# A fused adaLN block: w_qkv as one transfer of whole rows, w_in by halves of its rows, both folds transposed ahead of the modulation, and a new order of all steps

## The chip, the cores and the metric

The kernel runs on one core of a Trainium2 chip. A core has five engines that run their own instruction queues side by side: TensorE (PE, matmuls and their weight loads), VectorE (DVE), ScalarE (ACT), GpSimd (POOL) and SyncE (SP, which here only issues transfers). Transfers are moved by 16 DMA engines; a transfer stands in the queue of the engine that issues it (SP or ACT here). Engines wait for each other through semaphores. The metric is the device time of one execution in microseconds (us); all times below are in us unless marked ns.

## What is computed

Two blocks on a sequence of 2048 tokens with 448 features, each behind a layer norm that is modulated by a conditioning vector c, and gated into the residual:

```
mod = silu(c) @ w_mod                     # six vectors of 448: sa ca ga sb cb gb
h = layernorm(x) * (1 + ca) + sa
q, k, v = split(h @ wqkv)                 # 16 heads of 28
phi(t) = [softmax(t @ w_phi), softmax(-(t @ w_phi))]        # per head
kv = phi(k)^T v ;  z = sum over tokens of phi(k)
o = phi(q) kv / (phi(q) z + 1e-6)
x = x + ga * (o @ wo)
h = layernorm(x) * (1 + cb) + sb
z1, z2 = split(gelu(h @ w_in))            # 896 columns each
g = w_sp @ layernorm(z2) + b_sp           # mixes over the 2048 tokens
x = x + gb * ((z1 * g) @ w_out)
```

All inputs are bfloat16; sums are kept in float32.

## The kernel before

The program has a fast path, which is what runs here, and a general path behind a flag that is read near the end; nothing of the general path runs. In the fast path (`fast_path`) the 2048 tokens are 16 tiles of 128. Its steps are small Python functions, each of which issues a few instructions for one tile or one block, and a string, `ORDER`, lists every step of the whole program in the order of issue. An engine's queue is just the steps of that string that use it, in that order. A word is a step's name, its numbers, the engine where there is a choice (`/V` VectorE, `/S` ScalarE, `/G` GpSimd, `/Y` SP) and the PSUM bank that it writes (`@A0` to `@A2` are pairs of banks, `@B0`, `@B1` single ones). There are only these five, so a step that wants a bank waits until the step that reads its last content is done.

The program has these stages:

- **The head.** `ld:` words issue the loads: tiles of x (`x0` to `x5`), w_qkv, the columns of w_mod for the shift and scale of the first block (`wsa`, `wca`), `phi`. `du` issues warm-up matmuls on zeros (lines 720 to 725), whose result nobody reads. `ct` and `ce` turn c into a column and take its silu. `csA`/`ccA` multiply it with w_mod into the columns of the shift and the scale (`esA`/`ecA` copy them out of PSUM). The modulation is not applied to the tokens but folded into the weights, and w_phi is folded into the q and k parts of w_qkv: `FTk`/`FTq` transpose the raw k and q weights on TensorE (16 transposes of 112x112 each), `ETk`/`ETq` copy them out, `PFk`/`PFq` multiply them with the block-diagonal w_phi (`bd`), `EPk`/`EPq` scale the rows by 1 + ca on the way out of PSUM. `FSk`/`FSq` and `FCk`/`FCq` make the row that the shift adds. For v, `SHv` makes the shift's row and `SCv` scales the weights in place. `X` and `XE` turn the first four normalised tiles on TensorE; later tiles are turned by transposing transfers (`T1`).
- **Keys and values.** Per tile, layer norm statistics on VectorE (`l1s`: L843, L844), then `kM`, `vM` (matmuls), the two exponentials on ScalarE (`kF`, `kE`), the sums and reciprocals on VectorE (`kS`, `kR`), the normalisation (`kP`), and `kA`, which adds the tile into the 16 small key-value products. `qM`, `qE`, `qF` make the features of q for 512 tokens at a time. `gr` and `ge` make the gates' rows.
- **The middle.** Per tile, `nM` (numerator and denominator), `nX`, `nC`, `nS`, `nT`, `nA` (division and sum of the two halves), a transposing transfer `T2`, `wM`/`wN` (times wo), `wR` (evacuates and adds the residual), `wQ` (squares), the second layer norm `l2R`, `l2r`, `l2a` for pairs of tiles, a transposing transfer `T3`, and then the first product of the second block: `zM` (z2, with `zG` gelu, `zQ` squares, `zR`, `zW`, `zN` normalisation) and `yM` (z1 for 512 tokens and 128 columns, with `yG` gelu). `SHw` and `SCw` fold shift and scale into w_in. `wN` is `wM` with one more matmul (line 994) that adds x through the identity, so that ScalarE can evacuate; without it, `wR` on VectorE adds x.
- **The token mix.** `P` steps multiply w_sp (loaded transposed by the `W` transfers) with z2, seven products where eight blocks would be plain, with sums of blocks prepared by `sS` and `tT`; `d` and `x` evacuate on VectorE and GpSimd; `oM`, `oE`, `oD` multiply with w_out, add the residual and store.

The steps that the change and the prediction touch are `FTk`/`FTq` (from line 801), `ET`, `PF`, `EP`, `SH`, `SC`, `load_rows` (line 642), the table of loads (line 650) and `ORDER` (line 482).

## Time and profile before

| | before |
|---|---|
| median of 3 runs | 253.3 (252.15 to 253.48) |
| the profiled execution: its own time | 252.36 |
| its span (first to last instruction) | 250.5 |
| DMA moved in the span | 25.2 MB |
| HBM read, written | 8.87 MB, 1.84 MB |

The span ends when the last store has landed. In the rows of a timeline stand the start, the duration, the engine, the line, the operation with its tiles and the number of instructions merged into the row; in brackets, how long the engine idled before it and who released it. [...] In the rows of windows, for each stretch, stand the length, the busy time and the count of instructions for PE, PEld (weight loads), DVE, ACT and POOL, the granted TensorE clock (1.00 is full), the mean busy share of the DMA engines, and GB/s.

### The profile page before, as it was taken

The page shows a single profiled execution, that of the slowest core. Times are in us where ns is not written, and L with a number is a line of the kernel's source. Part 1 is how long each engine was busy: PE and PEld are TensorE (multiplying, and loading weights), DVE is VectorE, ACT ScalarE, POOL GpSimd, SP SyncE. Part 2 cuts the span into 40 slices and gives each one's busy share as a digit, 9 for nine tenths or more (in the row PEclk, how much of TensorE's full clock was granted, in tenths as well). Part 3 has the DMA queues.
Part 4 walks back from the last instruction along what each step waited for, and adds up shares of the span by engine and source line. Part 5 has one row for each costly group of instructions (what it writes and reads, how often), then busy time and mean ns, then how long its engine had stood idle before and what let it go on. Part 6 is the DMA issues. An engine that isn't in the chain of part 4 may idle for free.

```text
span 250.5 us, 4157 instructions
## 1 busy us (share of the span) xinstructions
PE 243.3 (97%) x1517; PEld 127.0 (51%) x1517; DVE 185.4 (74%) x371; ACT 104.2 (42%) x220; POOL 125.2 (50%) x166
## 2 busy tenths in 40 slices
PE   7999999999999999999999999999999999999993
...
PEclk9889999999999999999999999999999999999999
...
GB/s 176 267 245 154 104 111 257 178 190 1 94 155 139 153 125 177 131 145 219 136 171 1 179 160 41 3 0 0 0 3 38 0 0 3 55 0 37 18 79 82
DMA packets 68655, 25.22 MB, mean 101 GB/s; under 512 B 58129, under 2 KB 68498, under 8 KB 68626
## 3 DMA queue, kind: packets, MB, share of 16 engines
...
HBM read 8.87 MB, written 1.84 MB: 43 GB/s over the span
## 4 chain that ended last, share of the span: by engine, by line
PE 77%; DVE 12%; POOL 4%; DMA 3%; issue 1%; ACT 1%; DVEq 0%; POOLq 0%
PE g_ps L1115 29%; PE o_ps L1150 8%; PE z_ps L1069 7%; PE z_ps L1040 7%; PE g_ps L1136 6%; PE x_ps L996 3%; DVE f_ksum L891 3%; PE v_ps L885 3%; DVE f_st L843 3%; PE k_ps L877 2%; PE q_ps L932 2%; PE kvacc L908 2%; PE num L960 2%; PE warm_ps L725 2%; DMA f_hT<-f_xpad 2%; DMA f_ar<-f_ar 1%
## 5 line engine op out<-in xcount | busy, mean ns | idle before, releaser
L1124 DVE TENSOR_TENSOR f_zb<-g_ps,f_zb 128x512 f32<-128x512 f32 (+1 forms) x31 | 20.3, 668 | 18.5 <-PE g_ps L1115 18.1
L1115 PEld LDWEIGHTS <-f_z2n 128*128 128x128 bf16 x192 | 18.8, 98 | 22.5
L1131 POOL TENSOR_TENSOR f_z1T<-f_zb,f_z1T 128x512 bf16<-128x512 f32 (+1 forms) x11 | 12.0, 1102 | 35.6 <-DVE f_zb L1124 35.6
L1040 PE MATMUL z_ps<-f_ar,f_hT 112*128 112x448 bf16 (+1 forms) x128 | 26.7, 352 | 0.5 <-DMA f_hT<-f_xpad 0.5
L1069 PE MATMUL z_ps<-f_hT,f_ar 113*128 113x512 bf16 (+1 forms) x112 | 26.4, 378 | 0.1
L1150 PE MATMUL o_ps<-f_wout,f_z1T 128*128 128x448 bf16 x112 | 22.5, 352 | 0.0
L1115 PE MATMUL g_ps<-f_ar 128*128 128x512 bf16 x96 | 22.2, 379 | 0.0
L1131 POOL TENSOR_TENSOR f_z1T<-f_Sx,f_z1T 128x512 bf16<-128x512 f32 x6 | 7.3, 1221 | 26.4 <-DVE f_Sx L1124 26.4
L937 ACT ACTIVATE f_Eq<-q_ps 112x1024 bf16<-112x1024 f32 x16 | 16.2, 1037 | 6.5 <-PE q_ps L932 6.5
L1072 ACT ACTIVATE f_z1T<-z_ps 128x512 bf16<-128x512 f32 x28 | 15.9, 594 | 6.0 <-PE z_ps L1069 5.8
L1040 PEld LDWEIGHTS <-f_hT 112*128 112x128 bf16 (+1 forms) x128 | 11.9, 97 | 12.8 <-DMA f_hT<-f_xpad 2.0
L1044 ACT ACTIVATE f_zb<-z_ps 128x896 bf16<-128x896 f32 x16 | 14.6, 915 | 6.8 <-PE z_ps L1040 3.7
L980 DVE TENSOR_TENSOR f_ar<-num,f_w 128x896 bf16<-128x896 f32 x16 | 17.1, 1087 | 0.5
L1069 PEld LDWEIGHTS <-f_ar 113*128 113x128 bf16 (+1 forms) x112 | 10.8, 97 | 12.9 <-issue 0.4
L880 ACT ACTIVATE f_E<-k_ps 128x448 bf16<-128x448 f32 x32 | 16.0, 558 | 2.7 <-DVE f_phik L898 2.0
L891 DVE TENSOR_REDUCE f_ksum<-f_E 128x32 f32<-128x896 bf16 x16 | 16.6, 1051 | 0.1
L1115 PE MATMUL g_ps<-f_Eq,f_z2n 128*128 128x512 bf16 x72 | 16.7, 379 | 0.0
L1150 PEld LDWEIGHTS <-f_z1T 128*128 128x128 bf16 x112 | 10.9, 98 | 10.7
L1153 DVE TENSOR_TENSOR f_xpad<-o_ps,f_x 128x448 bf16<-128x448 f32 x16 | 9.8, 620 | 8.0 <-PE o_ps L1150 6.8
L877 PE MATMUL k_ps<-f_Wk,f_hT 113*128 113x448 bf16 (+1 forms) x64 | 15.4, 366 | 0.0
L1115 PEld LDWEIGHTS <-f_ar 128*128 128x128 bf16 x96 | 9.4, 98 | 11.2
L932 PE MATMUL q_ps<-f_hT,f_Wq 113*128 113x512 bf16 (+1 forms) x64 | 15.0, 379 | 0.0
...
## 6 DMA issues: line engine op xcount, KB each, us to landing
...
f_ar<-in_B_w_in_dram ACTq DMA_DIRECT2D x2, 784.0 KB, 5.8
...
f_x<-in_A_x_dram SPq DMA_DIRECT2D x2, 448.0 KB, 8.8
f_wmg<-in_w_mod_dram ACTq DMA_DIRECT2D x2, 392.0 KB, 4.3
f_wout<-in_B_w_out_dram SPq DMA_DIRECT2D x1, 784.0 KB, 5.8
...
f_x<-in_A_x_dram ACTq DMA_DIRECT2D x1, 448.0 KB, 7.3
```

The lines of the kernel that those rows point to most:

```text
L877: nc.tensor.matmul(t[:, 0, 0:D], lhsT=hT[0:KR[m], i, m, :], rhs=Wk[0:KR[m], m, :], start=(m == 0), stop=(m == KC - 1))
L880: nc.scalar.activation(out=Er[i % NR][:, s, :], in_=ps["k" + str(i)][:, 0, 0:D], func=ACT.Exp, scale=1.0 - 2.0 * s)
L891: nc.vector.tensor_reduce(out=ksum[:, i], in_=Er[i % NR][:].rearrange("p s (c f h) -> p (s c) h f", c=4, h=HP), axis=AX.X, op=ALU.add)
L932: nc.tensor.matmul(t[:, u, :], lhsT=Wq[0:KR[m], m, cc * CB:cc * CB + P], rhs=hT[0:KR[m], 4 * st:4 * st + 4, m, :], start=(m == 0), stop=(m ...
L937: nc.scalar.activation(out=Eq[st // 2][0:CB, 2 * c2:2 * c2 + 2, s, (st % 2) * 512:(st % 2 + 1) * 512], in_=ps["q" + str(n)][0:CB, :, :], f ...
L980: nc.vector.tensor_tensor(out=tr[i % 2][:], in0=numv(i)[:, :, :, 0:DH], in1=wr[i // 2 % 2][:, i % 2].unsqueeze(3).to_broadcast([P, 2, H, D ...
L1040: nc.tensor.matmul(t[:, hf, 0:D], lhsT=hT[0:KR[m], i, m, :], rhs=win_s[0:KR[m], m, FH + hf * D:FH + (hf + 1) * D], start=(m == 0), stop=(m ...
L1069: nc.tensor.matmul(t[:, 0, :], lhsT=win_s[0:KR[m], m, fc * P:(fc + 1) * P], rhs=hT[0:KR[m], 4 * st:4 * st + 4, m, :], start=(m == 0), stop ...
L1115: nc.tensor.matmul(g, lhsT=sta[:, m, :], rhs=mov[:, m, :], start=(m == 0 and i in (1, 6, 7)), stop=(m == 7), skip_group_check=True)
L1124: nc.vector.tensor_tensor(out=o, in0=x, in1=y, op=ALU.add)
L1131: eng.tensor_tensor(out=z, in0=T[r][:, c0:c1], in1=z, op=ALU.mult)
L1150: nc.tensor.matmul(ps["o" + str(t)][:, 0, 0:D], lhsT=later["z1T"][:, FO[n], t * P:(t + 1) * P], rhs=wout_s[:, FO[n], :], start=(n == 0), s ...
```

## The change

Three loads (`wk`, `wv`, `wq`: 392 KB each, pieces of 896 bytes out of rows of 2688) become one, `wqkv` (1176 KB, whole rows), into one tile of which the three old names are views. The two halves of w_in are halves of its rows (`win0` the first two blocks of 112 rows with all 1792 columns, `win1` the other two), not halves of its columns. The step `dm` (nine small dummy matmuls in the middle) is gone. `wM` adds the identity matmul exactly when ScalarE evacuates; there are four such tiles now, and were seven. The string `ORDER` is new from the first word to the last.

```diff
-ORDER = """du:2@A1 ld:wk/S ld:x1/Y l1s:1 l1e:1,2/V l1r:1,2 tbl du:3@A2 ld:c/S du:3@A0 m1/G ld:x0/Y ld:wsa/Y m2a/V du:3@B1 du:14@A1 m4 ld:phi/Y du:3@B0 l1s:0 ct@B0
...
+ORDER = """ld:x0/S l1s:0 du:1@A0 m2b/V m1/G du:2@B1 du:1@B0 du:1@A1 du:2@B0 du:1@A0 du:1@A1 du:8@A2 l1e:0,1/V l1r:0,1 l1a:0/V tbl du:8@A1 ld:c/S ld:wqkv/Y ct@A2 ce:1
+ce:2 ce:3 m4 ce:4 du:4@B0 du:2@B0 ld:wsa/Y ld:phi/Y FTq:1@A1 FTk:1@B1 FTk:0@A2 ETk:1/V ld:x1/Y FTq:0@B0 ETq:1/S ld:wca/Y csA@A0 du:1@B1 du:2@B1 m3 du:1@A1
...
-    wk_raw = aph.tile([P, KC, D], BF, name="f_wk_raw")
-    wq_raw = aph.tile([P, KC, D], BF, name="f_wq_raw")
-    wv = aph.tile([P, KC, D], BF, name="f_wv")
+    wqkv = aph.tile([P, KC, 3 * D], BF, name="f_wqkv")
+    wq_raw, wk_raw, wv = (wqkv[:, :, n * D:(n + 1) * D] for n in range(3))
...
-        "wk": lambda q: load_rows(q, wk_raw[0:CB], A_wqkv[:, D:2 * D]),
-        "wv": lambda q: load_rows(q, wv[0:CB], A_wqkv[:, 2 * D:3 * D]),
-        "wq": lambda q: load_rows(q, wq_raw[0:CB], A_wqkv[:, 0:D]),
+        "wqkv": lambda q: load_rows(q, wqkv[0:CB], A_wqkv),
...
-        "win0": lambda q: load_rows(q, win_s[0:CB, :, 0:FH], B_w_in[:, 0:FH]),
-        "win1": lambda q: load_rows(q, win_s[0:CB, :, FH:2 * FH], B_w_in[:, FH:2 * FH]),
+        "win0": lambda q: load_rows(q, win_s[0:CB, 0:2], B_w_in[0:2 * CB]),
+        "win1": lambda q: load_rows(q, win_s[0:CB, 2:4], B_w_in[2 * CB:]),
...
-    def dm(n, i):
-        for _ in range(n):
-            nc.tensor.matmul(ps["n" + str(i)][:, 1, 480:512], lhsT=zero[:, 0:P], rhs=zero[:, 0:32], start=True, stop=True)
...
-"wM": lambda i, slot: wM(i, slot, False), "wN": lambda i, slot: wM(i, slot, True),
+"wM": lambda i, slot, eng: wM(i, slot, eng is nc.scalar),
```

What this does to the engines' queues is seen at three places. The first is the start of SP's queue, the loads. Before (f_wm1 are the columns of w_mod, first shift, then scale):

```order
L655 DMA f_x_74<-in_A_x_dram 128x448
L654 DMA f_x_74<-in_A_x_dram 128x448
L650 DMA f_wm1_117<-in_w_mod_dram 112x4x464
L647 DMA f_phi_114<-in_A_w_phi_dram 112x4x28
L656 DMA f_x_74<-in_A_x_dram 128x2x448
L650 DMA f_wm1_117<-in_w_mod_dram 112x4x464
L643 DMA f_wv_113<-in_A_wqkv_dram 112x4x448
L643 DMA f_wq_raw_112<-in_A_wqkv_dram 112x4x448
L657 DMA f_x_74<-in_A_x_dram 128x4x448
```

The same place now:

```order
L643 DMA f_wqkv_111<-in_A_wqkv_dram 112x4x1344
L650 DMA f_wm1_115<-in_w_mod_dram 112x4x464
L647 DMA f_phi_112<-in_A_w_phi_dram 112x4x28
L655 DMA f_x_74<-in_A_x_dram 128x448
L650 DMA f_wm1_115<-in_w_mod_dram 112x4x464
L656 DMA f_x_74<-in_A_x_dram 128x2x448
L657 DMA f_x_74<-in_A_x_dram 128x4x448
```

All of w_qkv goes first on SP (the k part had been first on ScalarE's queue), and the columns of w_mod, w_phi and all tiles of x but the first (which moved to ScalarE's queue) stand behind it.

The second place is VectorE's queue around the scale of the first block, f_ca1. Before, from the silu (f_scol) on (a few rows between are left out in both):

```order
L749 TENSOR_TENSOR f_scol_132<-f_e_131,ct_ps_212 112x4
L843 BN_STATS f_st1_143<-f_x_74 128x6
L844 BN_AGGR f_mv1_139<-f_st1_143 128x2
L767 CAST f_Ga_118<-cf_ps_255 112x4
L694 COPY f_Gb_119<-f_ident_73 112x112
L815 CAST f_wTk_135<-fs_ps_285 112x4
L764 TENSOR_SCALAR f_ca1_134<-cf_ps_305 112x4
L787 TENSOR_SCALAR f_Wk_109<-pf_ps_324,f_ca1_134 112x448
L787 TENSOR_SCALAR f_Wk_109<-pf_ps_347,f_ca1_134 112x448
L787 TENSOR_SCALAR f_Wk_109<-pf_ps_335,f_ca1_134 112x448
L787 TENSOR_SCALAR f_wv_113<-f_wv_113,f_ca1_134 112x448
```

The same place now (f_wTk and f_wTq are the transposed raw weights, f_st0 and f_st1 the statistics of tiles of x):

```order
L747 TENSOR_TENSOR f_scol_130<-f_e_129,ct_ps_199 112x4
L813 COPY f_wTk_133<-tps_234 112x2x448
L692 COPY f_Ga_116<-f_ident_73 112x112
L765 CAST f_Ga_116<-cf_ps_265 112x4
L813 COPY f_wTq_134<-tps_254 112x2x448
L762 TENSOR_SCALAR f_ca1_132<-cf_ps_325 112x4
L841 BN_STATS f_st1_141<-f_x_74 128x6
L842 BN_AGGR f_mv1_137<-f_st1_141 128x2
L841 BN_STATS f_st0_140<-f_x_74 128x6
L785 TENSOR_SCALAR f_wqkv_111<-f_wqkv_111,f_ca1_132 112x448
L785 TENSOR_SCALAR f_Wk_109<-pf_ps_393,f_ca1_132 113x448
```

VectorE copies both folds' transposes out ahead of the scale; between the scale and its share of the v weights stand the statistics of two tiles, and it evacuates one of the eight fold results instead of three.

The third place is ScalarE's queue from the silu of c on. Before:

```order
L813 COPY f_wTk_135<-tps_220 112x2x448
L813 COPY f_wTk_135<-tps_243 112x2x448
L813 COPY f_hT_75<-xt_ps_279 128x512
L783 ACTIVATE f_Wk_109<-pf_ps_341,f_ca1_134 113x448
L659 DMA f_x_74<-in_A_x_dram 128x4x448
L783 ACTIVATE f_wv_113<-sh_ps_353,f_ca1_134 113x448
L783 ACTIVATE f_wv_113<-f_wv_113,f_ca1_134 112x448
L880 ACTIVATE f_E0_121<-k_ps_361 128x448
```

Now, from the scale's first use to the first exponential (f_E0):

```order
L781 ACTIVATE f_wqkv_111<-sh_ps_307,f_ca1_132 113x448
L811 CAST f_wTk_133<-fs_ps_346 112x4
L781 ACTIVATE f_Wk_109<-pf_ps_320,f_ca1_132 112x448
L781 ACTIVATE f_Wk_109<-pf_ps_315,f_ca1_132 112x448
L781 ACTIVATE f_Wq_110<-pf_ps_383,f_ca1_132 112x448
L781 ACTIVATE f_Wk_109<-pf_ps_388,f_ca1_132 112x448
L886 CAST f_vaug_124<-v_ps_399 128x16x28
L811 CAST f_wTq_134<-fs_ps_417 112x4
L781 ACTIVATE f_Wq_110<-pf_ps_408,f_ca1_132 112x448
L811 COPY f_hT_75<-xt_ps_443 128x512
L811 COPY f_hT_75<-xt_ps_458 128x512
L781 ACTIVATE f_Wq_110<-pf_ps_449,f_ca1_132 113x448
```

Before, the first exponential of the keys stood right behind the scaled v weights, and the q fold came later, between the exponentials; now all but one of the fold results of k and q, and two turned tiles, stand ahead of it.

90 lines of the change are left out of this document (45 added, 45 removed).

## The prediction

> **What bounds the kernel now.** I read the page's busy shares and slices first, then TensorE's timeline row by row, then the windows of the places where it loses time, then the transfers and the groups by line.
>
> ```profile
> PE 243.3 (97%) x1517; PEld 127.0 (51%) x1517; DVE 185.4 (74%) x371; ACT 104.2 (42%) x220; POOL 125.2 (50%) x166
> ...
> PE   7999999999999999999999999999999999999993
> ...
> PEclk9889999999999999999999999999999999999999
> ```
>
> TensorE is full in every slice but the first and the last, so the end is its first useful matmul, plus the work, plus whatever it loses on the way: idle time, filler matmuls and time at a lowered clock. The dip of the clock in slices 2 and 3 is the only one. The timeline of TensorE shows the losses one by one (start, duration, line, count, idle before it):
>
> ```profile
> 1.23 4.74 PE L725 MATMUL warm_ps<-f_zero 128*128 128x256 bf16 x28 [1.23 <-DVE f_zero L683]
> ...
> 6.27 0.62 PE L809 MATMUL tps<-f_ident,f_wk_raw 112*112 112x112 bf16 x8
> ...
> 8.20 0.54 PE L760 MATMUL cf_ps<-f_scol,f_wm 112*128 112x1 bf16 x16 [0.58 <-DVE f_scol L749]
> ...
> 11.16 1.68 PE L774 MATMUL sh_ps<-f_wv,f_Ga 112*128 112x448 bf16 x4
> 12.62 1.70 PE L877 MATMUL k_ps<-f_Wk,f_hT 113*128 113x448 bf16 x4
> 14.12 1.21 PE L809 MATMUL tps<-f_ident,f_wq_raw 112*112 112x112 bf16 x16
> ...
> 15.39 0.93 PE L877 MATMUL k_ps<-f_Wk,f_hT 113*128 113x448 bf16 x4
> 16.15 0.94 PE L826 MATMUL fs_ps<-f_Ga,f_wq_raw 112*112 112x1 bf16 x16
> ...
> 38.32 0.59 PE L908 MATMUL kvacc<-f_vaug,f_phik 128*128 128x116 bf16 x8 [0.35 <-DVE f_phik L898]
> ...
> 112.66 1.69 PE L1040 MATMUL z_ps<-f_ar,f_hT 113*128 113x448 bf16 x8 [0.25 <-DMA f_hT<-f_xpad]
> ...
> 116.27 1.69 PE L1040 MATMUL z_ps<-f_ar,f_hT 113*128 113x448 bf16 x8 [0.20 <-DMA f_hT<-f_xpad]
> ...
> 235.45 10.76 PE L1150 MATMUL o_ps<-f_wout,f_z1T 128*128 128x448 bf16 x56
> ```
>
> Useful work starts at 6.27 (the first fold transposes; what precedes is filler and the tiny transposes of c) and ends at 246.2. Four matmuls with 448 columns take 0.76 from start to start at full clock (15.39 to 16.15). The two groups at 11.16 and 12.62 take 2.96 instead of 1.52: the clock was halved there, and with part of the transposes behind them that is a loss of **1.6**. Waits lose 1.1 before 11.2 (0.58 for the silu of c, and handovers of some 0.1 each), 0.5 around 38.3, and some 1.9 between 60 and 118 in pieces like the last two bracketed ones. Behind 138 there is nothing to win:
>
> ```profile
> 138.00:246.30 108.30, 108.21 (x515) 50.13 (x513) 70.76 (x98) 2.06 (x4) 38.41 (x23) 1.00 0.16 38
> ```
>
> TensorE (first figure behind the length) is busy for 108.21 of 108.30.
>
> **The change, part by part.** The sum is made in the profiled execution, 252.36 (span 250.5), which lies 0.9 under the median of the three runs; I add the same difference to the median.
>
> *Where the work starts.* Before, the k part of w_qkv came alone and first; now the folds wait for all of it.
>
> ```profile
> f_wk_raw<-in_A_wqkv_dram ACTq DMA_DIRECT2D x1, 392.0 KB, 4.3
> f_wv<-in_A_wqkv_dram SPq DMA_DIRECT2D x1, 392.0 KB, 6.1
> f_wq_raw<-in_A_wqkv_dram SPq DMA_DIRECT2D x1, 392.0 KB, 7.2
> ...
> f_ar<-in_B_w_in_dram ACTq DMA_DIRECT2D x2, 784.0 KB, 5.8
> ...
> f_x<-in_A_x_dram SPq DMA_DIRECT2D x1, 448.0 KB, 8.0
> ```
> ```profile
> 0.72 0.42 ACTq L643 DMA_DIRECT2D f_wk_raw<-in_A_wqkv_dram  x1
> ...
> 5.00 0.31 SPq L643 DMA_DIRECT2D f_wv<-in_A_wqkv_dram  x1
> 5.35 0.49 SPq L643 DMA_DIRECT2D f_wq_raw<-in_A_wqkv_dram  x1
> 5.89 0.68 SPq L657 DMA_DIRECT2D f_x<-in_A_x_dram  x1
> ...
> 47.12 0.33 ACTq L643 DMA_DIRECT2D f_ar<-in_B_w_in_dram  x1
> ...
> 49.86 0.32 ACTq L643 DMA_DIRECT2D f_ar<-in_B_w_in_dram  x1
> ```
>
> Issue plus time to landing: k at 5.0, v at 11.1, q at 12.6, the next 448 KB of x at 13.9. By 5.0, 392 KB of weights and the first 112 KB of x are in. Now 1176 KB of w_qkv and 112 KB of x must be in: 784 KB more. A half of w_in is just 784 KB, and its second half landed 2.7 behind the first; by the rows of v and q (392 KB in 1.5) it is 2.9, by that of x (448 KB in 1.3) 2.3. So it lands between 7.3 and 7.9; rows of 2688 bytes have no row here, the nearest are w_in's 1792, and x, whose rows lie one behind the other as these do, is faster: I take **7.5**, and 7.0 to 8.1 for the range. Filler covers TensorE up to about 6.5 (31 of the warm-up matmuls stand ahead, against 28 in 4.75), then it idles. Start: **+1.2**. All loads behind it on SP move back too: by the same rates the shift columns land near 9.1, x's second tile at 9.6, the scale columns (949 KB behind w_qkv) near 11.1 and the third and fourth tile at 12, where before they were all in by 9.6.
>
> *Filler.* Forty-one warm-up matmuls for 28; ten of them stand behind the landing and are paid for at full clock, some 0.1 each: **+1.0**. The other 31 lie under the wait. Nine small ones in the middle go, and three of seven identity matmuls that add the residual:
>
> ```profile
> 64.16 0.19 PE x_ps L994
> ...
> 67.92 0.22 PE num L965 x9
> ```
>
> That is **−0.2** and 3 x 0.19 = **−0.6**; the residual is then added by VectorE while it evacuates, which it does for 9 of the 16 tiles already.
>
> *The clock and the old waits.* With the transposes of both folds in one run, and warm-up matmuls between the small ones, TensorE streams more in 7.5 to 14.6. If the clock stays up, **−1.6**. The old head waits go as well, **−1.1**: the tiny transposes of c stand behind 25 warm-up matmuls instead of 28, so its silu is done before 8, and the shift columns that use it aren't reached before 9.2.
>
> *New waits.* Followed by hand with the durations below, from 7.5: 32 transposes to 9.2, the shift columns, six warm-up matmuls, one turned tile, the shift product and two fold products to 11.8, so the scale columns are waited for by nobody. Scales exist at 12.4.
>
> ```profile
> L843 DVE BATCH_NORM_STATS2 f_st<-f_x 128x6 f32<-128x448 bf16 x16 | 9.8, 612 | 2.0 <-DMA f_x<-in_A_x_dram 1.9
> ...
> L783 ACT ACTIVATE f_Wq<-pf_ps,f_ca 112x448 bf16<-112x448 f32 x3 | 1.9, 636 | 0.0
> ```
>
> On VectorE two tiles' statistics (0.6 and 0.2 each) and two small steps stand between the scale and its share of w_v, so v of tile 0 starts at 14.6 instead of 14.2: 0.4. ScalarE then has ten evacuations in a row (six fold results and two turned tiles at about 0.6, one v, one small column), and every bank that TensorE wants next is behind one of them: its first exponential comes at 19.2, against 14.36 before. That costs TensorE 0.6 in four pieces up to 21, and as much again in handovers and behind the gate rows and the q exponentials up to 36. **+1.6**, between 0.7 and 3. At 36 the changed kernel is then 1.2 + 1.0 − 1.6 − 1.1 + 1.6 = 1.1 behind. The wait at 38.3 came from VectorE being late with the statistics between the key sums; those are done earlier now: **−0.5**.
>
> *The middle, 55 to 118.* The new order hands work from VectorE on: four tile sums and three normalisations of z go to GpSimd, three squares of z to ScalarE.
>
> ```profile
> 80.00:118.00 38.00, 37.40 (x216) 18.81 (x217) 32.71 (x96) 29.07 (x70) 26.29 (x49) 1.00 0.87 154
> ```
> ```profile
> L986 DVE TENSOR_TENSOR f_ar<-f_ar 128x448 bf16<-128x448 bf16 x11 | 4.6, 425 | 0.1
> ...
> L986 POOL TENSOR_TENSOR f_ar<-f_ar 128x448 bf16<-128x448 bf16 x5 | 5.2, 1050 | 14.5 <-DVE f_ar L980 14.5
> ...
> L1010 DVE SCALAR_TENSOR_TENSOR f_ar<-f_zb 128x896 bf16<-128x896 bf16 x6 | 7.3, 1219 | 6.6 <-ACT f_zb L1044 6.6
> ...
> L1063 DVE TENSOR_SCALAR f_z2n<-f_zb,f_zm,f_zv 128x896 bf16<-128x896 bf16 x9 | 4.2, 503 | 0.6 <-POOL f_zv L1026 0.6
> ...
> L1063 POOL TENSOR_SCALAR f_z2n<-f_zb,f_zm,f_zv 128x896 bf16<-128x896 bf16 x7 | 8.0, 1138 | 0.4
> ```
>
> VectorE is the fullest of the helpers (32.7 of 38) and loses 4 x 0.43 + 3 x 1.22 + 3 x 0.50 = 6.9; GpSimd (26.3 of 38) gains 4 x 1.05 + 3 x 1.14 = 7.6. Of the 1.9 of waits I take a quarter as gone, **−0.5**; the bounds are −1.9 and, if GpSimd falls behind, +3.
>
> *w_in by rows.* They move, like half of the gate weights and the last tiles of x, from ScalarE's queue to SP's, whose issues take 0.3 to 0.7 each and wait for nobody in between but the transposes of xn. Both halves are now needed by the first product that uses them. My estimate from their place behind the last of those transposes is an issue near 40 and 46 and, with 5.8 to land, both there by 53; the product comes near 58. It costs nothing, and one for one if SP is late by over 5.
>
> Sum: +1.2 + 1.0 − 0.2 − 0.6 − 1.6 − 1.1 + 1.6 − 0.5 − 0.5 = **−0.7**: 251.7 in the profiled execution, **252.6** for the median.
>
> **The clock as a rival.** Stretches of 3.41 between the changes of the granted clock:
>
> ```profile
> 4.36:7.77 3.41, 3.20 (x39) 2.72 (x37) 2.66 (x13) 1.02 (x3) 2.96 (x12) 1.00 1.16 261
> 7.77:11.18 3.41, 2.98 (x69) 2.87 (x69) 3.14 (x13) 1.57 (x4) 2.33 (x6) 1.00 1.12 261
> 11.18:14.59 3.41, 3.41 (x15) 1.70 (x14) 1.91 (x5) 1.94 (x4) 2.38 (x4) 0.50 1.10 316
> ```
>
> TensorE was busy for 2.98 of 3.41 in the second stretch, and the third was halved all the same: nearly all of its 69 matmuls have one column or are transposes, and little streams. In the changed kernel a stretch that holds the wait for w_qkv, the 32 transposes and the shift columns looks like that one, unless transposes count as streaming; so may 11.3 to 14.7, with two groups of one-column matmuls. Then 3.41 at half clock follow, with some 1.3 of streaming in them: +1.3, **253.9**. [...]
>
> **Other rivals.** *The helpers catch up:* w_qkv at 7.2, half of the new head waits, and the middle without gaps would give −0.3 − 0.8 − 1.4 more than the sum; with a little over half of it, **251.2**. For it speaks VectorE's relief; against it the ten evacuations in a row on ScalarE. *GpSimd becomes the bound of the middle:* a tile's sum there takes 1.05 for 0.43, each pair then goes through its moments, power and normalisation, all on GpSimd, and the last pair's transposes are what TensorE already waits for at 112.66 and 116.27. With most of the 7.6 falling in 80 to 118, GpSimd is at some 85% there. From the point where the last pair is over 1 late, lateness is paid one for one, since only z1 products are left to fill in: two pairs late by 1.2 each, some 2.6 over the sum: **255.2**. *The one transfer is no faster:* at v's and q's rate w_qkv lands at 7.9, +0.4, within the forecast.
>
> **How the numbers follow.** Forecast (251.9 to 253.4) 0.40, helpers catch up 0.24, clock falls 0.18, GpSimd 0.18. The range that leaves out 0.2 reaches from 250.9 to 255.1. Half a per cent, about what a measurement of this kernel can tell from no change, is 1.3: under 252.0 counts as faster (0.24 and the low edge of the forecast: 0.29), over 254.6 as slower (GpSimd, and the clock together with a late landing: 0.22), 0.49 between.
>
> **What would show it.** Right: the first fold transpose at 7.3 to 7.9, no halved clock behind it, ScalarE's first exponential near 19, key 8 of 16 finished about 1 later than before, no idle over 0.3 at 38, and the last o matmuls ending near 245.5. Wrong: a halved stretch between 8 and 18; a wait for the scale columns; fold results waited for by more than 3 in all; GpSimd named as the releaser of the last transposes of hT.

## The result: 0.6% slower, and the profile after

The changed kernel takes 254.31 us (median of 17 runs, 253.54 to 255.89), the kernel before 253.18 beside it (17 runs, 251.28 to 256.13): a ratio of **1.0062, 95% interval 1.0041 to 1.0083**. The forecast was 252.6, 0.3% faster; the time lies inside the range of 250.9 to 255.1, on the other side of no change. Profiled, the changed kernel took 253.92 (span 252.1) against 252.36 (span 250.5): 1.56 more, and 1.65 more in the span. The time of the kernel before goes with its clock: of its 29 runs beside c1 below, those with a mean granted clock of 0.995 or more have a median of 252.15, those of 0.991 to 0.993 (one halved stretch, as in the profile that the prediction read) 252.7, and eight of 0.984 to 0.986 lie at 255.1 to 256.0, most of which the ratios leave out, like any run over 1.5% above the fastest of its kernel.

The page of the changed kernel, busy time by engine and the slices of TensorE and of its clock:

```profile
PE 243.6 (97%) x1509; PEld 127.2 (50%) x1518; DVE 185.0 (73%) x360; ACT 107.3 (43%) x229; POOL 118.0 (47%) x168
...
PE   8999999999999999999999999999999999999992
...
PEclk9999999999999999999999999999999999999999
```

The dip of the clock in slices 2 and 3 has gone, and TensorE is as full as before. So the loss has to be found in TensorE's timeline again (start, duration, count, and in brackets the idle time ahead; rows overlap, so what a row costs is read from start to start: the one at 9.83 lasts 0.54, and the next starts 0.40 behind it):

```profile
7.99 2.00 PE L807 MATMUL tps<-f_ident,f_wqkv 112*112 112x112 bf16 x32
9.83 0.54 PE L758 MATMUL cf_ps<-f_scol,f_wm 112*128 112x1 bf16 x16
10.23 0.81 PE L723 MATMUL warm_ps<-f_zero 128*128 128x256 bf16 x4
11.10 0.38 PE L865 MATMUL xt_ps<-f_ident,f_xpad 128*128 128x128 bf16 x4
11.32 0.38 PE L723 MATMUL warm_ps<-f_zero 128*128 128x256 bf16 x2
11.76 0.92 PE L772 MATMUL sh_ps<-f_wqkv,f_Ga 112*128 112x448 bf16 x4
...
14.16 0.60 PE L723 MATMUL warm_ps<-f_zero 128*128 128x256 bf16 x4
14.81 0.36 PE L834 MATMUL pf_ps<-f_BD,f_wTq 112*112 112x112 bf16 x4
...
43.91 0.93 PE L875 MATMUL k_ps<-f_Wk,f_hT 113*128 113x448 bf16 x4 [0.53 <-DMA f_hT<-f_xpad]
...
143.10 0.61 PE L1109 MATMUL g_ps<-f_ar 128*128 128x512 bf16 x2 [0.22 <-DVE f_ar L1087]
...
236.59 11.03 PE L1144 MATMUL o_ps<-f_wout,f_z1T 128*128 128x448 bf16 x56
```

The fold transposes start at 7.99, against 6.27. Two fillers start at 11.32, 0.11 apart, and would be through 0.22 later; what follows starts 0.44 later. The four at 14.16 should hand on at 14.60; the next product starts at 14.81. There are four such gaps of 0.22 behind fillers, one of them between two filler steps. No bracket shows them, since TensorE counts as busy to the end of its last matmul. At 43.91 there is a wait that before did not have, 0.69 from start to start; at 143.10 and among the last o matmuls (11.03 for 56, against 10.76) two more.

These are the marks of TensorE (starts in us, from the timelines) of the runs that follow. K/V end is the last key/value sum; in kernels with the changed head the scale columns of block B (0.4) are already done there.

```
                    folds  shift product  K/V end  token mix  last o   span
before               6.27     11.16        54.69    138.43    245.86   250.5
b1 (before again)    6.11     11.50        55.05    139.17     246.50   251.3
changed              7.99     11.76        56.38    139.26    247.26   252.1
c1 (changed again)   8.65     12.27        57.07    140.51    248.18   252.7
e5 filler banks      8.60     11.57        56.62    139.85    247.89   252.8
e6 turns first       8.36     11.99        55.91    139.28    246.93   251.6
e9 both              8.21     11.31        55.05    138.50    246.13   250.8
e11 k, q first       7.86     10.79        54.63    137.99    245.78   250.4
e12 identity back    6.91     10.69        54.72    139.23    247.06   251.7
e10 ScalarE relieved 8.50     12.13        56.88    145.13    253.29   257.9
e14 before, 1 load   8.40     15.93        59.14    143.11    250.67   255.2
```

The start of one kernel moves by 0.7 between two executions (7.99 and 8.65), with the landing of w_qkv. The twelve profiles that have the one transfer on SP land it at 7.95 to 8.83, with a median of 8.3, so the first profile shows the earliest of them. Differences along a row are surer than those down a column.

### The profile page after: what moved, and what is told of

The parts are those of the page before. It is cut to its first block, busy times and chain, and to the rows that moved or that the text cites. A ratio compares the mean times of both kernels' runs of the same rounds, so it can differ in the third digit from the quotient of the medians.

```text
span 252.1 us, 4152 instructions
## 1 busy us (share of the span) xinstructions
PE 243.6 (97%) x1509; PEld 127.2 (50%) x1518; DVE 185.0 (73%) x360; ACT 107.3 (43%) x229; POOL 118.0 (47%) x168
## 4 chain that ended last, share of the span: by engine, by line
PE 59%; POOL 15%; DVE 8%; DMA 7%; ACT 5%; issue 4%; POOLq 0%; DVEq 0%; SPq 0%; ACTq 0%
PE g_ps L1109 29%; PE o_ps L1144 6%; PE g_ps L1130 4%; PE z_ps L1034 4%; POOL f_z2n L1057 3%; DMA f_wqkv<-in_A_wqkv_dram 3%; PE v_ps L883 2%; POOL f_zv L1020 2%; PE q_ps L930 2%; DMA f_hT<-f_xpad 2%; POOL f_xpad L852 2%; PE x_ps L990 2%; DVE f_st L841 2%; PE num L958 2%; PE k_ps L875 2%
## 5 line engine op out<-in xcount | busy, mean ns | idle before, releaser
L1125 POOL TENSOR_TENSOR f_z1T<-f_zb,f_z1T 128x512 bf16<-128x512 f32 (+1 forms) x9 | 9.8, 1102 | 70.7 <-DVE f_zb L1118 70.7
L980 POOL TENSOR_TENSOR f_ar<-f_ar 128x448 bf16<-128x448 bf16 x9 | 9.4, 1049 | 19.6 <-DVE f_ar L974 17.2
L990 PE MATMUL x_ps<-f_ar 112*128 112x448 bf16 x64 | 14.4, 352 | 0.2 <-DMA f_ar<-f_ar 0.2
```

What stands on the lines that cost most here:

```text
L990: nc.tensor.matmul(t[:, 0, 0:D], lhsT=oT[0:CB, i % 4, cc, :], rhs=wo_s[0:CB, cc, :], start=(cc == 0 and not with_x), stop=(cc == KC - 1))
```

## Experiments

Every ratio is against the kernel before, run beside it on the same chip.

**e5, e6: filler and turns.** e5 puts the same ten fillers into banks that the next step does not use; e6 moves two transfers up on SP.

```diff
 e5
- du:1@B1 du:2@B1 m3 du:1@A1   X:0@A1 ... du:2@A0 ... SHv@A0 ... du:4@A2 ... PFq:1@A2 PFk:3@B1 PFk:0@A0
+ du:4@B1 m3                   X:0@A1 ... du:2@B1 ... SHv@A0 ... du:4@A2 ... PFk:3@B1 PFk:0@A0 PFq:1@A2
 e6
- ld:wout/Y ... W:0,7 ... T1:14,16 ... T1:12,14
+ T1:12,14 T1:14,16 ld:wout/Y W:0,7
```

> The changed kernel with the same ten warm-up matmuls behind the landing of w_qkv, but in banks that the next useful step does not use: four in one group and two in the same bank after the turned tile, and the last four ahead of two k products, with the q product that uses their bank put behind these. Theory A, the four gaps of 0.22 behind the filler groups in the trace are handovers of a bank from TensorE to itself, and paid in full: filler costs 2.0, of which 0.9 goes: the first v matmul 0.7 to 0.9 earlier than 15.43, and the end 0.6 to 0.9 earlier, 253.5. Theory B, the gaps lie beside waits for the evacuations on ScalarE and VectorE: the gaps turn into waits for these, no change within 0.3.

> The changed kernel with the last two transposes of hT for the K/V phase (tiles 12 and 13 first, then 14 and 15) issued on SP ahead of w_out's load and of one w_sp transpose. Theory A, the wait of 0.69 at 43.0 comes from the place of these on SP's queue, and TensorE is the bound behind it: that wait goes, the K/V end is 0.6 to 0.7 earlier, and so is the end of the program: 253.6. Theory B, the phase is paced by the helpers (exponentials, feature sums): the wait goes, but comes back as gaps before 57, or in the middle: end earlier by under 0.2, 254.2.

e5: 253.74, ratio 1.0023 (0.9994 to 1.0051). e6: 253.70, ratio 1.0023 (0.9994 to 1.0053). Both ratios lie some 0.4% under the changed kernel's, and their intervals just touch its interval. TensorE's timeline of e5:

```profile
10.70 0.60 PE L724 MATMUL warm_ps<-f_zero 128*128 128x256 bf16 x4
11.13 0.39 PE L866 MATMUL xt_ps<-f_ident,f_xpad 128*128 128x128 bf16 x4
11.36 0.38 PE L724 MATMUL warm_ps<-f_zero 128*128 128x256 bf16 x2
11.57 0.92 PE L773 MATMUL sh_ps<-f_wqkv,f_Ga 112*128 112x448 bf16 x4
...
13.97 0.60 PE L724 MATMUL warm_ps<-f_zero 128*128 128x256 bf16 x4
14.41 0.58 PE L835 MATMUL pf_ps<-f_BD,f_wTk 112*112 112x112 bf16 x8
```

Four fillers now take 0.43 to the next start (10.70 to 11.13), two take 0.21. In the trace of the changed kernel the first matmul of a step whose bank the step just ahead on TensorE has filled starts 0.06 after the end of the last matmul there, which is 0.33 after its start (five places from 7.1 to 14.9, each behind fillers of 256 columns). A first matmul into another bank starts 0.11 after it there (10.67 to 10.78), and so do the matmuls of one step into one bank (the four fillers at 13.97 of e5: 0.44 to the next start). Theory A holds for the head: the fillers cost 1.1 + 0.9. In this profile the wait at 43 grew to 1.27 and took most of it back, since the last transposes landed no earlier (43.2, against 43.0 in the changed kernel). That wait is e6's. In the changed kernel SP issues the transfers in this order:

```profile
34.17 0.57 SPq L671 DMA_DIRECT2D f_wout<-in_B_w_out_dram  x1
34.80 1.87 SPq L1071 DMA_TRANSPOSE f_wsp<-in_B_w_sp_dram  x1
37.31 3.02 SPq L857 DMA_TRANSPOSE f_hT<-f_xpad  x2
...
f_hT<-f_xpad SPq DMA_TRANSPOSE x4, 4.8
```

The last row is that of the transfers from 30 to 45: four transposes of hT, with a median of 4.8 from issue to landing. In e9 (e6's order, below) it is this:

```profile
35.76 2.60 SPq L858 DMA_TRANSPOSE f_hT<-f_xpad  x2
38.42 0.65 SPq L672 DMA_DIRECT2D f_wout<-in_B_w_out_dram  x1
...
f_hT<-f_xpad SPq DMA_TRANSPOSE x4, 3.3
```

Issued 1.5 earlier, and without 784 KB and a w_sp transpose ahead of them, they land 1.5 sooner after their issue (by the median). The wait at 43 is gone in e6 and e9, theory A of e6: from the shift product to the K/V end e6 takes 43.92, against 44.62 in the changed kernel and 44.80 in c1. Since e6 moves both transfers, it does not tell which of the two held the transposes up.

**c1, e9, e11: does it add up, and does it last?** e9 is e5 and e6 together, with one more word moved (the last half sum of z1 ahead of the evacuation of output tile 12). e11 is e9 with w_qkv in three transfers: k, q, then the shift columns, then v. c1 is the changed kernel again.

```diff
 e9 (beside e5's and e6's)
- oM:12,0,7@B0 oE:12 x:1,2,8,256,512/V
+ x:1,2,8,256,512/V oM:12,0,7@B0 oE:12
 e11 (beside e9's)
- ld:wqkv/Y ... ld:wsa/Y ld:phi/Y FTq:1@A1 FTk:1@B1 FTk:0@A2 ETk:1/V
+ ld:wk/Y ld:wq/Y ... ld:wsa/Y ld:wv/Y ld:phi/Y FTk:1@B1 FTk:0@A2 ETk:1/V FTq:1@A1
```

> The changed kernel once more, as the measure for the three beside it: 0.4 to 0.8% over before.

> The changed kernel with the filler in other banks and the two transposes of hT first on SP together, and the last half sum of z1 ahead of the evacuation of output tile 12. Theory A, the four handovers (0.9), the wait at 43.0 (0.7) and the wait at 244.3 (0.3) are paid one by one: 1.5 to 1.9 under the changed kernel run beside it, that is 0.1 to 0.4% under before. Theory B, the middle is paced by its helpers and transposing transfers, so that what is won ahead of 58 comes back as waits up to 118: the K/V end 1.3 to 1.6 earlier, the first product of the token mix less than 0.6 earlier, and the end under 0.9 earlier.

> The kernel with other filler banks, early transposes of hT and the early half sum, and w_qkv by three transfers: k, q, then the shift columns, then v, then the rest. Theory A, what the whole transfer costs is the late shift columns: they land near 8.4 instead of 9.5, their matmuls start there instead of 9.8, and the first v matmul comes 0.6 to 1.2 earlier than without; the end 0.5 to 1 earlier than without. Theory B, the scale columns (11.6) and the tiles of x bound the head, since as many bytes stand ahead of them as before: v and k start within 0.3 of the kernel without, and so does the end.

c1: 254.73, ratio 1.0053 (1.0015 to 1.0091). e9: 252.93 (252.26 to 253.24), ratio 1.0006 (0.9981 to 1.0031): 1.8 under c1 by the medians, and its longest run is shorter than c1's shortest (254.03). That is theory A. By the marks e9 is 2.02 ahead of c1 at the K/V end, 2.01 at the token mix and 2.05 at the last o (0.44 of it an earlier landing): what is won ahead of 58 stays. The moved word adds nothing that these runs show: the wait at 244.3 is absent in c1, e6 and e15 too, which do not move it. e11: 252.19, ratio 0.9977 (0.9937 to 1.0016): the shift columns start 0.5 earlier than in e9, and so does all that follows up to the token mix. Run again as e11b:

> The kernel with k and q first, other filler banks, early transposes of hT and the early half sum, once more, as the measure for the one beside it and to settle whether it is faster than before: 252.2 and 0.2% under before, the interval decides.

253.05, ratio 0.9989 (0.9960 to 1.0018). It makes up the whole loss; that it is faster than before is not shown. It also lost the clock in four of its 14 runs (mean clock of 0.976 to 0.985, 255.9 to 257.8), which none of the changed kernel's 17 did (0.995 or more in each).

**e4: three transfers in the place of the one.**

```diff
- ld:wqkv/Y ... FTq:1@A1 FTk:1@B1 FTk:0@A2 ETk:1/V
+ ld:wk/Y ld:wq/Y ld:wv/Y ... FTk:1@B1 FTk:0@A2 ETk:1/V FTq:1@A1
```

> The changed kernel with w_qkv by three transfers in its place on SP, k first, then q, then v, and the k transposes ahead of the q transposes. Theory A, bytes land in the order in which they are issued: k near 5.5, q near 6.8, v near 8; the transposes start near 6.9 instead of 8.0, but the shift columns still land near 9.5 and their matmuls start there, so only 0.2 to 0.4 is gained: 254.0. Theory B, the transfers share the queue and all land near 8, or the two more issues delay what is behind them: no change or up to 0.5 more. Theory C, short rows are slower: v lands near 9, and so do the shift columns, later: 0.5 to 1 more.

254.35, ratio 1.0076 (1.0056 to 1.0096). Issued at 0.72, 1.18 and 1.70, k lands at 5.1, q at 6.7, v at 8.3; the one transfer landed at 7.95 in the first profile and at up to 8.83 in others, so these traces show no difference that the shape of the rows makes. The early k is of no use, since the shift columns land as late as ever (TensorE's timeline of e4):

```profile
6.85 0.57 PE L810 MATMUL tps<-f_ident,f_wqkv 112*112 112x112 bf16 x8
7.86 1.40 PE L810 MATMUL tps<-f_ident,f_wqkv 112*112 112x112 bf16 x24 [0.43 <-DVE f_scol L750]
9.94 0.20 PE L761 MATMUL cf_ps<-f_scol,f_wm 112*128 112x1 bf16 x2 [0.69 <-DMA f_wm<-in_w_mod_dram]
```

The transposes begin 1.1 earlier than in the changed kernel and the shift columns 0.1 later. That is why e11 puts v behind them.

**e3, e14: filler and the granted clock.** e3 takes all ten fillers behind the landing out of the changed kernel. e14 is the kernel before with only the one transfer, first on SP.

```diff
 e3
- du:1@B1 du:2@B1 ... du:1@A1 ... du:2@A0 ... du:4@A2
 e14 (kernel before)
- ld:wk/S ld:x1/Y ... ld:wv/Y ... ld:wq/Y
+ ld:x1/S ld:wqkv/Y
```

> The changed kernel without the ten warm-up matmuls behind the landing of w_qkv. Theory A, they are paid for one by one and the clock stays up without them: the first key matmuls 0.9 to 1.1 earlier, 253.3. Theory B, they are what keeps the gate open: a stretch of 3.41 at half clock between 8 and 18, and with the filler saved the time is 0.3 to 0.8 above the changed kernel, 254.6 to 255.1. Theory C, they only fill waits for the scale columns and for ScalarE's evacuations: no change within 0.3.

> The kernel before with w_qkv as whole rows by the one transfer, now first on SP, and the first tile of x that it loads on ScalarE's queue ahead of c, as in the changed kernel; its order is otherwise kept, with 28 warm-up matmuls and none behind the landing. Theory A, start and end go together: the first fold transposes at 7.9 to 8.6 instead of 6.3, the end 1.3 to 2 later than before, with the clock as in before. Theory B, the old head has slack behind its halved clock: the transposes as late, the first keys and the K/V end under 0.8 later. Theory C, the idle time ahead of 8 closes the gate for two stretches: K/V end 2.5 to 4 later and a mean clock under 0.99.

e3: 254.37, but from 252.62 to 257.35; ratio 1.0082 (1.0051 to 1.0113). Its three runs with a mean clock of 0.999 or more took 252.6 to 253.4, less than the changed kernel; with a clock of 0.975 it took 257. Its windows between the changes of the granted clock (length, busy time of TensorE, its weight loads, VectorE, ScalarE, GpSimd, granted clock, share of the DMA engines, GB/s) in the profiled run, one with the low clock:

```profile
10.60:14.02 3.42, 2.89 (x53) 2.38 (x51) 2.80 (x10) 1.42 (x4) 1.83 (x5) 1.00 1.11 313
14.02:17.43 3.41, 3.41 (x27) 2.52 (x25) 3.27 (x12) 2.76 (x6) 3.30 (x6) 0.50 1.39 230
17.43:20.85 3.42, 3.42 (x30) 2.92 (x30) 1.41 (x5) 1.98 (x5) 2.27 (x5) 0.50 0.92 249
20.85:24.26 3.41, 3.41 (x14) 1.60 (x12) 2.05 (x6) 2.62 (x6) 3.20 (x5) 0.50 0.13 36
```

and those of the changed kernel, with the first of c1:

```profile
6.16:9.57 3.41, 3.23 (x40) 2.37 (x39) 2.47 (x14) 1.08 (x2) 1.69 (x8) 1.00 1.14 256
9.57:12.98 3.41, 3.24 (x50) 2.34 (x47) 2.46 (x8) 1.49 (x2) 1.64 (x4) 1.00 1.11 306
...
6.05:9.46 3.41, 2.52 (x29) 1.69 (x28) 2.37 (x13) 0.33 (x2) 1.48 (x8) 1.00 1.12 240
```

In e3, three stretches at half clock follow the one from 10.60; in the changed kernel none is halved. So theories A and B both hold, in different runs: the fillers cost 2.0 in the trace (0.9 to 1.7 by the runs of e3 that kept the clock), and without them the clock is lost in five of eleven runs. e14 took 257.29, ratio **1.0206** (1.0172 to 1.0239), theory C:

```profile
4.36:7.77 3.41, 1.98 (x19) 1.45 (x16) 1.80 (x9) 0.17 (x1) 0.75 (x2) 1.00 1.06 266
7.77:11.18 3.41, 1.41 (x20) 1.20 (x21) 2.42 (x7) 1.24 (x2) 2.32 (x12) 1.00 1.16 240
11.18:14.59 3.41, 3.12 (x54) 3.02 (x54) 2.42 (x11) 1.15 (x2) 2.21 (x5) 0.50 1.10 292
14.59:18.00 3.41, 3.41 (x22) 2.24 (x22) 2.64 (x6) 0.97 (x2) 1.42 (x3) 0.50 0.32 74
```

Waiting for w_qkv idles TensorE in two stretches, and the two behind the second are halved: 2.1 late at the start has become 4.45 at the K/V end. By itself the one transfer costs 5 us in all. The changed kernel is only 1.7 late at the K/V end, with 0.4 more work done there, so the filler and the new order of the head, the price of which the prediction counted as loss, save some 3.2 of the 4.45.

The busy share does not tell which stretch loses the clock: c1's above kept it with 2.52 of 3.41 busy, e3's lost it with 2.89. What tells in these traces is how many columns stream in a stretch (a filler has 256, a transposed block of weights 112, a key matmul 448). At full clock, with 0.109 for 256, some 8,000 would fit (an estimate). Counted from the matmuls of the traces, in stretches of 3.41 that line up with the changes of the clock:

```
                     stretch   columns   of them in transposes   clock of the next
b1                    7.44      1,859           775                 half
before                7.77      2,409           512                 half
e8                    5.47      2,838            18                 half
e10                  88.93      3,312             0                 half
e14                   4.38      3,332             0                 full
e3                   10.60      3,366           212                 half
e8                    8.88      3,588         3,575                 full
c1                    6.05      3,732         1,680                 full
changed               6.16      4,981         3,027                 full
```

Over all 20 traces, every stretch with up to 3,312 columns was followed by half clock and every one with 3,588 or more by full clock, at whichever clock it ran itself. Between the two lie two that kept the clock (e13 and e14) and one that lost it (e3), and the edges of the stretches are sure to some 50 columns only. Transposes counted like other matmuls in e8 (an experiment on the token mix, below, whose fold transposes ran at half clock): its stretch at 8.88 has 3,575 of its 3,588 columns in them, and full clock behind it (its windows, and from its timeline the row of the transposes):

```profile
5.47:8.88 3.41, 2.00 (x17) 1.18 (x15) 1.96 (x10) 0.17 (x1) 0.95 (x4) 1.00 1.09 241
8.88:12.30 3.42, 3.42 (x46) 3.42 (x46) 2.04 (x8) 1.80 (x2) 1.66 (x5) 0.50 1.15 219
12.30:15.71 3.41, 3.24 (x52) 2.34 (x49) 1.47 (x5) 0.59 (x2) 1.01 (x3) 1.00 1.10 328
...
8.88 3.24 PE L808 MATMUL tps<-f_ident,f_wqkv 112*112 112x112 bf16 x32 [1.15 <-DMA f_wqkv<-in_A_wqkv_dram]
```

The 69 matmuls of before's stretch at 7.77 hold 2,409 columns, since 48 of them have one: by this count that is why, with 2.98 of 3.41 busy, half clock followed.

**e13**, the same with the transfer on ScalarE's queue in the place of k:

```diff
- ld:wk/S ld:x1/Y ... ld:wv/Y ... ld:wq/Y
+ ld:wqkv/S ld:x1/Y
```

> The kernel before with w_qkv as whole rows by the one transfer, in the place of the k part, and nothing else changed. Theory A, the start sets everything behind it: the first fold transposes near 8 instead of 6.3, the shift and scale columns later by as much, the end 1.3 to 1.9 later than before. Theory B, the old order has slack in the head (clock, loads of v and q that were waited for): the first transposes 1.7 later, the first keys 0.5 to 1 later, and the end under 0.8 later.

263.23, ratio 1.0408 (1.0355 to 1.0461), and no answer to its question, for a reason of its own:

```profile
8.29 0.48 ACTq L653 DMA_DIRECT2D f_c_row<-in_c_dram  x1
...
13.49 0.53 PE L734 MATMUL ct_ps<-f_one,f_c_row 1*112 1x1 bf16 x4 [7.52 <-DMA f_c_row<-in_c_dram]
```

The row of c, 0.9 KB, stands on the same queue behind the 1176 KB. Its issue began only at 8.29, against 1.24 in the kernel before, where 392 KB stood ahead of it, and it landed near 13.4; there nobody waited for it after 6. Why the issue came so late is not shown: on SP, the loads behind w_qkv were issued from 1.17 on.

**e7, b1: what was the halved clock worth?** e7 gives the kernel before ten fillers around its shift columns; b1 is the kernel before, profiled again.

```diff
- csA@B1 ... FSk@A0
+ du:4@B1 csA@B1 du:3@A1 ... FSk@A0 du:3@B0
```

> The kernel before with ten warm-up matmuls around its shift columns (four ahead of them where TensorE idles, three behind, three behind the small k shift column), so that the stretch ahead of 11.2 holds more streaming. Theory A, the halved clock at 11.2 to 14.6 costs before its whole 1.6: with the fillers' 0.3 to 0.7 paid the time falls by 0.9 to 1.3, 251.1 to 251.5 against a before of 252.4. Theory B, the halved stretch is mostly covered by waits for the loads of x and for the helpers, as the spans of runs of before with a mean clock of 1.000 (250.2 and 250.4) against those of 0.992 (250.5 to 251.1) say: it is worth 0.4, and with fillers paid the time is within 0.4 of before. Theory C, the clock is halved all the same: 0.5 to 1 more.

> The kernel before, profiled once more. The runs of before so far lie at 252.1 to 252.4 where their mean granted clock was 0.995 to 1.000, and at 252.5 to 253.0 where it was 0.990 to 0.993 as in the profile that the prediction read. If this execution has the full clock: theory A, the 1.6 of the halved stretch is on the path (first keys and K/V end 1.2 to 1.6 earlier than 54.7, span 249); theory B, it lies beside other waits, and 0.4 to 0.7 is left of it at the end: the K/V end or the first product of the token mix at most 0.8 earlier, and longer waits at 37.6 or between 60 and 118. If the clock is halved again, the marks agree with the first profile within 0.4.

b1 (253.08) had the halved stretch again and says nothing. e7's clock stays at 0.999, and it takes 254.42, ratio 1.0059 (1.0028 to 1.0090), more than any theory had. Its fold transposes start 0.9 late, and with ten fillers it is still 0.2 ahead of before at key 8 (33.04 against 33.24). If its fillers cost the 0.3 to 0.7 that were expected, the clock is worth 1.4 to 1.8 up to there, about the forecast. Then it waits where before hardly did:

```profile
84.72 1.03 PE L1070 MATMUL z_ps<-f_hT,f_ar 113*128 113x512 bf16 x4 [1.36 <-DMA f_hT<-f_xpad]
...
143.03 1.04 PE L1137 MATMUL g_ps<-f_Eq,f_z2n 128*128 128x512 bf16 x4 [0.99 <-DVE f_z2n L1064]
```

The first is a transpose of hT that took 4.7 to land, against 3.4 at the same place of the kernel before. Why a full clock brings before only 0.6 at the end is left open: e7's waits may be its own.

**e1, e10, e12: the middle.** e1 is the changed kernel up to the K/V end with before's order behind it; e10 gives six steps from ScalarE back to VectorE; e12 is e11 with before's seven identity matmuls.

```diff
 e1: ORDER of the changed kernel up to KV:0, then that of before (dm left out, ecB right behind csB)
 e10
- SCw:1,1/S wQ:2/S wQ:3/S wQ:14/S zQ:8/S zQ:12/S
+ SCw:1,1/V wQ:2/V wQ:3/V wQ:14/V zQ:8/V zQ:12/V
 e12 (beside e11's)
- wM:3/V wR:3/V wM:4/V wR:4/V wM:10/V wR:10/V wM:11/V wR:11/V wM:5/S wR:5/S
+ wM:3/S wR:3/S wM:4/S wR:4/S wM:10/S wR:10/S wM:11/S wR:11/S wM:5/V wR:5/V
```

> The changed kernel up to the last key/value sums, and from there on the order of before (seven identity matmuls again, the nine small fillers left out). Theory A, the changed order from the K/V end on gives its savings (0.6 for three identity matmuls) back by waits of its own: the token mix starts about 1.1 behind before's 138.4, the last o matmul starts about 1.1 behind 245.9, and the median is the changed kernel's within 0.4 or a little less (253.9 to 254.4). Theory B, those waits are handed down by the head (everything 1.3 late at the K/V end, transfers of w_sp in another state), so before's order pays them too, without the savings: 254.8 or more.

> The changed kernel with six steps of the middle back from ScalarE to VectorE: one scaling of w_in (1.05 there, 0.44 on VectorE), the squares of three tiles of x and of two of z (0.77 and 1.14 there). Theory A, ScalarE is what the middle waits for (three of four waits of TensorE name it): the waits at 66.8, 81.6 and 115.3 go or shrink, the first product of the mix comes 0.5 to 0.9 earlier. Theory B, ScalarE is named only because it comes last, the pairs' chains and the transposing transfers set the pace: the mix starts within 0.3 of 139.3. Theory C, VectorE falls behind: up to 1 later.

> The kernel e11b with the residual of tiles 3, 4, 10 and 11 added on TensorE again by an identity matmul and evacuated by ScalarE, and that of tile 5 by VectorE, which is the choice of before (seven such matmuls instead of four). Theory A, TensorE is the bound and the three matmuls were worth their 0.6: 0.5 to 0.7 more. Theory B, VectorE is what the middle waits for: it is relieved of three evacuations of 0.7, the waits between 60 and 118 shrink by more than the matmuls cost: 0 to 0.6 less. Theory C, ScalarE is: 0.8 to 1.5 more.

The waits of TensorE in the changed kernel from 9.5 to 139 (sum, times, longest):

```profile
PE k_ps L875 <- DMA f_hT<-f_xpad: 0.5, 1, 0.5
PE num L958 <- ACT f_Eq L935: 0.4, 1, 0.4
PE num L958 <- ACT f_zb L1038: 0.2, 1, 0.2
PE z_ps L1063 <- ACT f_z1T L1066: 0.2, 1, 0.2
PE x_ps L990 <- DMA f_ar<-f_ar: 0.2, 1, 0.2
```

Three of the four in the middle name ScalarE, and e10 is the run that this reading suggests. It took 258.52, ratio 1.0182 (1.0119 to 1.0244), theory C and far beyond it:

```profile
PE x_ps L991 <- DMA f_ar<-f_ar: 2.1, 2, 1.8
PE num L959 <- DVE f_ar L975: 1.2, 2, 1.0
PE num L959 <- ACT f_Eq L936: 0.4, 1, 0.4
```

The six steps take 4.5 on VectorE in this trace. It comes late with the tiles' weights and sums, their transposes go out late, and from the K/V end to the token mix TensorE takes 88.25, against 82.88 (83.45 in c1). Some 1.3 of that is a stretch at half clock behind the long wait (the table's stretch at 88.93, 3,312 columns). The 0.4 for ScalarE stays. So VectorE has no room for 4.5 more in the changed order, and theory A, that ScalarE is what the middle waits for, finds nothing for it here. That it was as close to the path in the order before, and that what the change took from it was needed to keep pace, is an inference.

e1, 255.37, ratio 1.0127 (1.0108 to 1.0146), is by its time theory B, but does not decide. Behind the changed head the old order takes 84.49 from the K/V end to the token mix, against 83.75 behind its own head (84.1 in b1), where it has 0.6 more work; but two waits of 0.4 and 0.3 in e1 stand at the seam of the two orders (58 to 61), beside one of 0.9 at 73.

e12 took 253.74, ratio 1.0034 (0.9998 to 1.0069), 0.45% or 1.1 over e11b; the intervals overlap. From the K/V end to the token mix it takes 84.5, against 83.4 in e11, in one profile each, and two profiles of one order differ by up to 0.6 there. The three identity matmuls are 0.6 of it. The rest is waits, although VectorE got less to do, as in theory C, by which ScalarE is what the middle waits for. So removing these matmuls did bring what it should.

**e2, e8: the token mix.** e2 has before's order from its first product on; e8 moves the second group of middle-tap products ahead of the products that wait at 142.5, and has e9's early half sum.

```diff
 e2: ORDER of the changed kernel up to gM:1, then that of before
 e8 (beside the half sum of e9)
- gM:1@B1 P:0,0,6 P:0,0,1 d:0,0,1 yG:3,4 P:0,1,1 gM:0@B0
+ gM:1@B1 yG:3,4 gM:0@B0 P:0,0,6 P:0,0,1 d:0,0,1 P:0,1,1
```

> The changed kernel up to the first product of the token mix, and from there on the order of before. Theory A, the waits of 0.39 at 142.5 and 0.28 at 244.3 belong to the new order of the token mix (copies of the last z columns on GpSimd, last sums split by halves and put on VectorE): from the first product of the mix to the last o matmul 107.4 to 107.5 as in before, against 108.0, and the span's tail behind it as in before; 0.6 to 0.8 less than the changed kernel, 253.5 to 253.7. Theory B, they come from what is late when the mix starts (last z tiles): the wait near 142 stays, and the time is the changed kernel's within 0.3.

> The changed kernel with two edits in the token mix: the second group of middle-tap products stands ahead of the first products that need VectorE's differences of the last z tiles, and the last half sum of z1 stands on VectorE ahead of the evacuation of output tile 12, which waits for an output transfer. Theory A, the waits of 0.39 at 142.5 and 0.28 at 244.3 are made by these two orders alone: both go, from the first product of the mix to the last o matmul 107.4 as in before, the end 0.6 earlier, 253.7. Theory B, VectorE is late by more than the wait shows, and they come back some products later: under 0.2.

e2: 255.92, ratio 1.0141 (1.0122 to 1.0160); its mix starts with a wait of 1.3 at the seam, which neither theory had, so it leaves open whose the waits are. e8: 255.48, ratio 1.0115 (1.0094 to 1.0135), slower than the changed kernel. The wait at 142.5 went, and came back larger:

```profile
156.35 1.89 PE L1110 MATMUL g_ps<-f_ar 128*128 128x512 bf16 x8 [0.80 <-DVE f_zb L1119]
...
167.14 3.18 PE L1110 MATMUL g_ps<-f_ar,f_z2n 128*128 128x512 bf16 x14 [0.27 <-DVE f_zb L1119]
```

The products that were put back feed sums on VectorE, which then are late for the banks. Its profiled execution also ran 3.41 at half clock in the head, ahead of these waits; its other runs, with a mean clock of 0.996 or more, still took 255.1 to 255.9.

**e15: w_in by columns again**, in the changed kernel's two places.

```diff
-        "win0": lambda q: load_rows(q, win_s[0:CB, 0:2], B_w_in[0:2 * CB]),
+        "win0": lambda q: load_rows(q, win_s[0:CB, :, 0:FH], B_w_in[:, 0:FH]),
```

> The changed kernel with w_in by halves of its columns again, in the same two places on SP. Theory A, the shape of these loads costs nothing, since they land ahead of the first product that uses them (56.0 against 59.4): the changed kernel's 0.4 to 0.8% over before, no wait of a w_in product for a load. Theory B, halves by rows sped up their landing: the second half lands over 3 later, and the products of w_in wait: 0.3 to 1 more.

254.34 (four runs), ratio 1.0083 (1.0054 to 1.0113), at the upper edge of the changed kernel's interval; the second half lands at 55.8, against 56.0, and no product waits for it. The shape of these loads has no part in the time that this run shows.

## Why the prediction was wrong

The sum term by term, in us, in the profiled executions:

```
                           forecast   came
start                        +1.2     +1.7
filler behind the landing    +1.0     +1.1, and 0.9 of bank handovers
clock                        -1.6     -1.5 in the profile, 0.6 between runs
old waits of the head        -1.1     -1.1
new waits of the head        +1.6      0
 = up to 36                  +1.1     +1.1
wait at 38.3                 -0.5     -0.5, and 0.7 at 43.0
fillers, identity matmuls    -0.8     -0.8
middle                       -0.5     +0.3
token mix                     0       +0.6
tail behind the last matmul   0       +0.2
sum                          -0.7     +1.65
```

"Came" up to 36 is the K/V end, 1.69 late, less the 0.4 of scale columns done earlier and less the 0.2 of the row that follows; the new waits are what is left. The middle is what TensorE waits between K/V end and mix, each start against its distance in a stream: 2.6 before, 2.9 now. The two second profiles give another split of the same loss (c1 against b1): 2.0 late at the K/V end, 0.7 won back to the mix, 0.3 lost in it, and 0.2 to 0.3 won behind the last o start, 1.4 in all. So the tail's +0.2 and half of the mix's +0.6 are not stable, and the middle is +0.5 in that pair.

- **Up to 36** the sum was right by luck: errors that cancelled. The start was mis-sized: +1.2 was forecast, and it came as +1.7, and as +2.5 in c1 against b1. W_qkv landed at 7.95 to 8.83 and mostly beyond the 8.1 that the prediction took as the end of its range, slower than by the rate of v and q (7.9), which the prediction set aside for 7.5. ScalarE's first exponential came at 19.4, as forecast, but TensorE was not held up by the ten evacuations ahead of it: 1.6 was forecast, and nothing came.
- **The price of the filler** failed: "some 0.1 each" is a filler's stream. The handover of the bank that the next step shares with it was put at nothing, and cost 0.9 more; e5 takes these gaps out of the head, and e9 keeps the gain to the end.
- **The wait at 38.3, −0.5**, failed as a gain: the wait went, and 0.7 came back at 43.0, because the last transposes of hT became late. The new order puts w_out and a w_sp transpose ahead of them on SP, and the prediction looked at SP's queue for w_in alone. e6 and e9 show the 0.7 and that it is paid at the end. These two steps, 0.9 and 0.7, are as much as the whole loss of 1.6: without them e9 takes what the kernel before takes (1.0006), and the rest of the change gains nothing.
- **The middle, −0.5**, did not come. By the measure of the table the waits there are 2.6 to 3.3 in five profiles of the old order, and 2.9 to 3.5 in eleven of the new one: if anything, they rose. The prediction took a quarter of the waits as gone because VectorE is relieved. e10 shows that VectorE has no room in the new order, so relieving it was no mistake; that the receivers, ScalarE above all (e12), ate the gain is argued and not shown. The identity matmuls' saving came.
- **"Behind 138 there is nothing to win"** was true, and read as "nothing to lose". The new order of the mix waits 0.39 at 142.5 for VectorE's differences of z tiles; waits of 0.28 to 0.39 stand there in all profiles of this order but one, and e8, which puts other products ahead of it, brought larger ones. The 0.28 at 244.3 comes and goes between profiles of kernels with the same order there. From the first product of the mix to the last o matmul, the new order takes 107.6 to 108.0, against 107.3 and 107.4.
- **The clock, −1.6**: the stretch was won in the profile, and the clock kept in all 17 runs (means of 0.995 or more; one of c1's twelve has 0.993), but the runs of before without a halved stretch, by their mean clock, end only 0.6 sooner than those with one. One profiled execution had shown one state of a clock that differs from run to run. By the mean clock of its runs (0.984 to 1.000 beside c1) the kernel before has none, one or two stretches of 3.41 halved (an estimate: one in 250.5 lowers the mean by 0.007).
- **Rivals.** The clock did not fall: the stretch from 6.16 to 9.57, with 27 transposes, 7 fillers and the 4 tiny transposes of c, was followed by a full clock. The prediction left open whether transposes count as streaming; by the columns above they do. Without its transposes this stretch held only 1,954 columns, and e8's at 8.88 only 13; both were followed by full clock, where 2,409 and 3,312 columns (before, e10) were followed by half clock. "GpSimd becomes the bound of the middle" had the sign. GpSimd is named by no wait of TensorE, but the chain of work that ended last runs through it for 15% of the span (12% in c1, 4% before), and ScalarE waits 2.6 for its normalisations; no run takes work off it, so this rival is not ruled out as a part of the middle. "The one transfer is no faster" held: e4's three transfers land as early.
- **The signs.** No stretch was halved, ScalarE's first exponential came at 19.4, key 8 came 0.6 late (1.1 in c1), nothing idled at 38: as forecast. The last o matmuls ended at 247.6 instead of 245.5. The second half of w_in was issued at 50.5 and landed at 56.0, three later than estimated, and its first product came at 59.4: still nobody waited.
